# One list schedule for all five engines of a delta-rule attention with a routed MLP behind it, keys left unnormalised

## The chip, the cores and the metric

The kernel runs on one core of one Trainium2 chip. The metric is device time in microseconds (us) of one execution, lower is better. Inside the core five engines run side by side, each through its own list of instructions in order: PE (matrix multiplication), DVE (vector), ACT (scalar and activation), POOL and SP. SP does nothing here but issue DMA transfers; ACT and POOL issue some too. An instruction that waits for another engine holds up everything behind it in its own list.

## What is computed

The reference has two parts. The first is a linear attention with a delta rule, over 4 batches x 8 heads, 768 tokens and a head size of 48:

```
k_n = k / (norm(k) + 1e-6)
for t in range(S):
    y[t]  = q[t] @ state
    v_old = k_n[t] @ state
    state = state + beta[t] * outer(k_n[t], v[t] - v_old)
```

The second is a "mixture of depths" on the result x (each batch 768 rows of 384): a score per token, the 128 tokens with the highest score go through an MLP, and the gated result is added to them.

```
scores = x @ w_gate
top    = the 128 highest scores of the batch
ye     = relu(x[top] @ w1) @ w2            # 384 -> 1024 -> 384
out[top] = x[top] + sigmoid(scores[top])[:, None] * ye
```

## The kernel before

**The chunks.** The tokens are cut into chunks of 64. A *unit* is one chunk of two batches (16 heads); there are 24 units, 12 for batches 0 and 1 and 12 for batches 2 and 3. Within a chunk the delta rule is a triangular system, solved by an explicit inverse; from chunk to chunk it is a recurrence on the state.

**prep(i)**, per unit: ACT squares the keys (`ksq`, L195), DVE sums them (L197) and with ACT's square root makes 1/(norm + 1e-6) (`rn`, L199 to L202), POOL scales the keys (`kn`, L206), PE turns queries and keys (`p_t`, L214), ACT takes the turned blocks out of PSUM (`kq`, L216), PE makes the products k.k and k.q (`p_g`, L223). ACT takes the first out (`g`, L228), DVE takes the second out times a triangular mask (`pt`, L229), and SP shifts half of g to other partitions by DMA (L237).

**eliminate(e)**, for four units together (a *block*; six of them): DVE turns g (L245), scales it by beta (L247), POOL cuts it to a triangle (L249), and DVE inverts it in 30 steps of two dependent instructions (L256, L260), scales (L263) and turns the result into `tt` (L267) and back into g (L273). **join** puts the 32x32 inverses together to 64x64 ones (`p_z` L288, `p_j` L298, with copies by ACT, two units at a time).

**recur(i)**, per unit, in the order of the chunks: `r = v - k.state` (PE L326, DVE L329), `w = inverse.r` (PE L339, ACT `wbd` L344), the new state (PE L350, ACT `s` L356), the output `p_y` (PE L369, L376). For every second unit ACT takes the output out (`x`, L385), SP writes it, POOL multiplies it with w_gate (`xw`, L388) and ACT sums it to the score (L390).

**depths(g)**, for two batches: the scores are spread over all partitions (L404 to L423), DVE counts for every token how many are higher (L435, L440), and the tokens of rank below 128 are picked (L448 to L464), gathered, sent through the MLP (L483, L492; 256 tokens of the two batches side by side in L483) and added back by an indirect DMA (L496).

**Order.** The Python code advances four generators (rec, elim, prep, moe) in turn, with a fixed number of ticks per unit; the tile framework orders each engine's list and hands out the buffers of its pools. Ahead of everything ACT issues 96 small transfers of beta (L138). The last call, `depths(NG - 1)`, stands behind all units.

Of the kernel before, what the change touches and what calls it, by code (L numbers as in the profile page):

```python
# [8 lines left out]
FP32 = mybir.dt.float32  # L9
# [6 lines left out]
P = 128  # L16
C = 64
HC = 32


@with_exitstack
def kernel(
# [30 lines left out]

    nc = tc.nc
# [22 lines left out]
    loads = ctx.enter_context(tc.tile_pool(name="loads", bufs=3))  # L77
    small = ctx.enter_context(tc.tile_pool(name="small", bufs=3))
    work = ctx.enter_context(tc.tile_pool(name="work", bufs=2))
    keep = ctx.enter_context(tc.tile_pool(name="keep", bufs=8))  # L80
    moe = ctx.enter_context(tc.tile_pool(name="moe", bufs=2))
    psum = ctx.enter_context(tc.tile_pool(name="psum", bufs=1, space=PSUM))

    def ps_inv(name):
        return psum.tile([P, 512], FP32, name=name, tag="inv", bufs=3)

    units = [(g, c) for g in range(NG) for c in range(NCH)]
    n = len(units)
# [5 lines left out]
    raw = {}  # L94

    KB = 3
    qraw = [const.tile([P, HP, GB, DP], FP32, name=f"q_raw{m}") for m in range(KB)]
    NKN = 9
    kns = [const.tile([P, HP, GB, DP], FP32, name=f"kn{m}") for m in range(NKN)]

    def load(i, name):
        g, c = units[i]
        if name == "q":
            t = qraw[i % KB]
            dst = t.rearrange("p r b d -> p b r d")[:, :, :, :D]
# [35 lines left out]
    nbt = const.tile([P, NE, HC], FP32, name="nbt")  # L141
    nc.scalar.activation(nbt, bt, AF.Copy, scale=-1.0)

    ones = const.tile([P, P], FP32, name="ones")
    nc.vector.memset(ones, 1.0)
    mask_u = const.tile([P, C], FP32, name="mask_u")
    for par in range(2):
        hs = slice(par * C, (par + 1) * C)
        nc.gpsimd.affine_select(out=mask_u[hs], in_=ones[hs, :C], pattern=[[1, C]],
                                base=0, channel_multiplier=-1,  # L150
                                compare_op=ALU.is_gt, fill=0.0)
# [443 lines left out]
```

## Time and profile before

| what | value |
|---|---|
| median of three runs (lowest, highest) | 535.78 us (533.94, 540.02) |
| the profiled execution, its own time | 534.48 us |
| its span, first to last instruction | 532.8 us |
| mean granted TensorE clock | 0.784 of 2.4 GHz |
| busy share: PE, DVE, ACT, POOL | 61%, 50%, 31%, 16% |

The profiled execution lies 1.3 us under the median, and 1.7 us of its time lie outside the span. No engine is busy all the time, so the shares of the whole span say little; the stretches have to be read one by one. With the ends of the six L267 instructions as marks (137.8, 171.8, 231.2, 288.8, 359.8 and 422.1 us) the span falls into a start, five blocks and an end.

### The profile page before, as it was taken

To read this page: it belongs to the slowest core of one execution; us is meant where nothing else is said; L and a number is where in the kernel's file an instruction comes from. 1 tells how busy PE (TensorE), PEld (TensorE's weight loads), DVE (VectorE), ACT (ScalarE), POOL (GpSimd) and SP (SyncE) were. 2 spreads that over 40 slices of the span, in tenths; PEclk is the share of its full clock that TensorE was granted. 3 is DMA by queue.
4 is the path that set the end of the run, shared out by engine and by line. 5 is a ranking of instruction groups with operands and counts; after the bars stand their busy time and mean duration, and the time that the engine had idled before them with its cause. 6 is when DMAs were issued, how large, how long until landed. Compare 5 with 4: busy or idle time off the path is not lost.

```text
span 532.8 us, 13538 instructions
## 1 busy us (share of the span) xinstructions
PE 322.5 (61%) x5652; PEld 273.4 (51%) x5652; DVE 264.5 (50%) x722; ACT 166.8 (31%) x378; POOL 84.6 (16%) x126
## 2 busy tenths in 40 slices
PE   0000027650498898869882849489997578512594
PEld 0000015430487797758772648477786567411472
DVE  0000023689979257961978196981268800076100
ACT  0000045431335545533642425252434333300120
POOL 6000021201003212111212110220311101300002
PEclk9999999555569959965975576699969758856599
DMA  3462003333123433342333212211302300000002
GB/s 56 82 221 46 2 15 64 61 69 70 24 50 84 77 65 54 85 99 54 85 64 78 49 32 49 52 37 20 66 18 66 78 2 33 30 0 15 16 0 30
DMA packets 110957, 27.92 MB, mean 52 GB/s; under 512 B 105584, under 2 KB 110320, under 8 KB 110896
## 3 DMA queue, kind: packets, MB, share of 16 engines
q1 hardware_dynamic: 108912, 25.39, 23.0%
q0 software_dynamic: 832, 1.57, 1.7%
q8 instruction: 44, 0.72, 0.5%
q10 hardware_dynamic: 1152, 0.10, 0.1%
q14 instruction: 17, 0.14, 0.1%
HBM read 18.38 MB, written 5.51 MB: 45 GB/s over the span
## 4 chain that ended last, share of the span: by engine, by line
PE 39%; DVE 25%; issue 17%; ACT 7%; POOL 5%; DMA 4%; SPq 2%; POOLq 0%; DVEq 0%; ACTq 0%
DVE a_tmp L256 5%; PE p_y L376 5%; DVE a L260 5%; DVE junk_r L435 5%; PE p_m L483 4%; PE p_r L339 4%; PE p_j L298 4%; PE p_s L350 3%; PE p_m L492 3%; PE p_t L214 3%; PE p_z L288 3%; PE p_g L223 3%; PE p_y L369 2%; DMA k_raw<-in_k_dram 2%; PE p_m L416 2%
## 5 line engine op out<-in xcount | busy, mean ns | idle before, releaser
L256 DVE TENSOR_TENSOR a_tmp<-a 128x30 f32<-128x30 f32 (+9 forms) x180 | 67.3, 374 | 6.7 <-POOL a L249 2.8
L260 DVE TENSOR_TENSOR a<-a,a_tmp 128x30 f32<-128x30 f32 (+9 forms) x180 | 64.2, 357 | 4.4
L214 PE MATMUL p_t<-ident,kn 128*128 128x128 f32 x96 | 21.1, 353 | 74.1 <-POOL kn L206 69.1
L206 POOL TENSOR_TENSOR kn<-k_raw,rn 128x192 f32<-128x192 f32 x48 | 26.1, 565 | 209.2 <-PE p_s L350 76.7
L197 DVE TENSOR_REDUCE rn<-ksq 128x8 f32<-128x384 f32 x24 | 13.2, 549 | 85.7 <-ACT ksq L195 85.7
L214 PEld LDWEIGHTS p_t<-ident,kn 128*128 128x128 f32 x96 | 14.3, 179 | 79.4 <-POOL kn L206 70.7
L288 PE MATMUL p_z<-tt,g 32*32 32x32 f32 x768 | 22.3, 225 | 39.2 <-DVE tt L267 39.2
L229 DVE TENSOR_TENSOR pt<-p_g,mask_u 128x256 f32<-128x256 f32 x48 | 18.9, 417 | 54.4 <-PE p_y L376 36.5
L376 PE MATMUL p_y<-wbd,pt 128*64 128x96 f32 x384 | 44.4, 278 | 1.5 <-ACT wbd L344 1.5
L339 PE MATMUL p_r<-r,tt 64*64 64x48 f32 x704 | 33.0, 241 | 16.8 <-DVE r L329 14.4
L376 PEld LDWEIGHTS p_y<-wbd,pt 128*64 128x64 f32 x384 | 40.7, 162 | 3.0 <-ACT wbd L344 1.9
L223 PE MATMUL p_g<-kq 48*64 48x128 f32 x768 | 37.6, 327 | 7.1 <-ACT kq L216 7.1
L288 PEld LDWEIGHTS p_z<-tt,g 32*32 32x32 f32 x768 | 20.0, 139 | 40.6 <-issue 31.9
L339 PEld LDWEIGHTS p_r<-r,tt 64*64 64x64 f32 x704 | 29.0, 154 | 19.7 <-DVE r L329 16.3
L388 POOL TENSOR_TENSOR xw<-x,wg 128x384 f32<-128x384 f32 x24 | 25.0, 1042 | 88.6 <-ACT x L385 79.8
L344 ACT COPY wbd<-p_r 64x384 f32<-64x384 f32 x48 | 22.7, 473 | 50.0 <-PE p_r L339 37.4
L216 ACT COPY kq<-p_t 128x512 f32<-128x512 f32 x48 | 27.4, 586 | 32.4 <-PE p_t L214 30.1
L223 PEld LDWEIGHTS p_g<-kq 48*64 48x64 f32 x768 | 28.9, 163 | 12.8 <-ACT kq L216 10.6
L350 PE MATMUL p_s<-wbd,kn 128*48 128x96 f32 x352 | 24.9, 299 | 11.6 <-ACT wbd L344 11.6
L369 PE MATMUL p_y<-s,kq 48*64 48x48 f32 x704 | 31.8, 231 | 0.0
L329 DVE TENSOR_TENSOR r<-v_raw,p_r 128x384 f32<-128x384 f32 x22 | 12.1, 548 | 38.0 <-PE p_r L326 38.0
L298 PE MATMUL p_j<-g 32*32 32x32 f32 x768 | 25.2, 230 | 8.4 <-ACT g L292 8.3
(79 smaller groups left out, 536.7 us busy)
## 6 DMA issues: line engine op xcount, KB each, us to landing
k_raw<-in_k_dram SPq DMA_DIRECT2D x96, 48.0 KB
q_raw<-in_q_dram SPq DMA_DIRECT2D x96, 48.0 KB
v_raw<-in_v_dram SPq DMA_DIRECT2D x96, 48.0 KB
out_dram<-x SPq DMA_DIRECT2D x24, 192.0 KB
w_sb<-in_moe_w_dram SPq DMA_DIRECT2D x2, 1536.0 KB
bt<-in_beta_dram ACTq DMA_DIRECT2D x96, 1.0 KB
g<-g SPq DMA_DIRECT2D x48, 32.0 KB
tt<-tt SPq DMA_DIRECT2D x12, 128.0 KB
```

What stands on the lines that cost most here:

```text
L214: nc.tensor.transpose(ps[:, r * P:(r + 1) * P], x[:, r].rearrange("p b d -> p (b d)"), ident)
L216: nc.scalar.copy(kq[:, :, o], ps.rearrange("p (r t) -> p r t", t=P))
L223: nc.tensor.matmul(ps[bb][hs, r], lhsT=kq[ds, r, 0, hs], rhs=kq[ds, r, :, hs], start=True, stop=True)
L256: nc.vector.tensor_tensor(out=t, op=ALU.mult, in0=a[:, j + 1:, j:j + 1].to_broadcast([P, w, j]), in1=a[:, j:j + 1, :j].to_broadcast([P, w, ...
L260: nc.vector.tensor_tensor(out=a[:, j + 1:, :j], in0=a[:, j + 1:, :j], in1=t, op=ALU.add)
L288: nc.tensor.matmul(ps[lo[par], b], lhsT=gt[hi[par], n0 + b, :HC], rhs=tt[hi[par], n0 + b, HC:], start=True, stop=True)
L298: nc.tensor.matmul(ps[lo[par], b], lhsT=gt[lo[par], n0 + b, HC:], rhs=gt[lo[par], n0 + b, :HC], start=True, stop=True)
L339: nc.tensor.matmul(pw[hs, bb, r], lhsT=tt[hs, ch * GP + r * GB + bb], rhs=rhs[hs, bb, r], start=True, stop=True)
L350: nc.tensor.matmul(p_s[bb * DP:bb * DP + D, r], lhsT=kn[:, r, bb, :D], rhs=wb[:, bb, r].rearrange("p h d -> p (h d)"), start=(c == 0 and r ...
L369: nc.tensor.matmul(p_y[bb][rows, h * D:(h + 1) * D], lhsT=kq[ds, r, 1, par * C:(par + 1) * C], rhs=s_old[ds, r, par], start=(h == 0), stop ...
L376: nc.tensor.matmul(p_y[bb][rows, r * 2 * D:(r + 1) * 2 * D], lhsT=pt[:, r, bb], rhs=wb[:, bb, r].rearrange("p h d -> p (h d)"), start=(c = ...
L435: nc.vector.tensor_scalar(out=junk[:, :e - a], in0=rows[:, a:e], scalar1=mine, scalar2=None, op0=op, op1=ALU.add, accum_out=count[:, j, o: ...
```

## The change

The kernel is written anew round the same blocks of arithmetic.

**Order.** Every step is entered into a `Plan` with its engine, a duration written by hand (in us), the steps that it depends on, a priority (lower goes first) and the ring buffers that it takes and gives back. A list scheduler runs through the engines and yields one order, in which the instructions are then emitted, with the framework's own reordering off. Buffers are fixed rings; which slot a step gets is decided in the plan.

**Keys unnormalised.** No step scales the keys ahead. The turned block of k.k has the squared norms on its diagonal; `turn_in`, `root` and `scales` take them from there once per block. The factors go into the matrix before the elimination (`bh`), into a triangular table made by POOL (`mb`), and into the values (`vh`, a DVE instruction of 384 elements per unit). `ksq`, `rn` and `kn` are gone.

**Other moves.** The masked block p is copied out by ACT and masked in place by POOL, with two AFFINE_SELECT of 64 partitions x 512 elements per unit. join goes unit by unit. The score is one DVE instruction per output tile. `depths` goes batch by batch, its MLP 128 tokens wide, with the counting in two stages (tiles 0 to 3, then 4 and 5). Loads use two transfers instead of four. beta comes in 24 transfers, four of them (for the first block) from ACT behind three loads, the others from SP.

```diff
...
+    def add(self, eng, dur, emit, deps=(), prio=0.0, take=(), give=(), lat=0.15):
...
+    def pick(self, free, ops):
...
+        first = min(at for at, _ in cand)
+        urgent = [(at, op) for at, op in cand if op.prio < -500]
+        fits = [(at, op) for at, op in cand if at <= first + 1e-9 and
+                all(at + op.dur <= u + 0.2 or op.prio <= o.prio for u, o in urgent)]
+        return min(fits or urgent, key=lambda c: (c[1].prio, c[1].seq))
...
+            for name, key in op.take:
+                slots = self.rings[name]
+                k = min(range(len(slots)), key=lambda x: slots[x])
+                slots[k] = float("inf")
+                self.slot[key] = (name, k)
+            op.start, op.end = at, at + op.dur
+            free[op.eng] = op.end
...
+            for key in op.give:
+                self.refs[key] -= 1
+                last[key] = max(last.get(key, 0.0), op.end)
+                if self.refs[key] == 0:
+                    name, k = self.slot[key]
+                    self.rings[name][k] = last[key] + 0.15
...
+        return sorted(done, key=lambda o: (o.start, o.seq))
...
-                            nc.scalar.dma_start(
-                                out=bt[p0:p0 + GP, g * (NCH // BC) + e],
-                                in_=beta_src[par, half, g, e, c])
+    ring("k", 10, [GP, DP])
+    ring("q", 3, [GP, DP])
+    ring("v", 3, [GP, D])
+    ring("kq", 9, [GI, 2, P])
+    ring("p", 9, [GP, C])
+    ring("g", 2, [NB, C])
...
+    rings["inv"] = [psum.tile([P, 512], FP32, name=f"inv{m}") for m in range(3)]
+    plan.ring("inv", 3)
+    rings["y"] = [psum.tile([P, 2, 512], FP32, name="py")]
+    plan.ring("y", 1)
...
+    def load_beta(eng, e):
+        for par in range(2):
+            for half in range(2):
+                p0 = (par * 2 + half) * HC
+                eng.dma_start(out=bt[p0:p0 + HC, e],
+                              in_=beta_src[par, half, e // (NCH // BC), e % (NCH // BC)])
...
-        nc.scalar.activation(ksq, kr.rearrange("p b r d -> p (b r) d"), AF.Square)
-        rn = small.tile([P, GP], FP32, name="rn")
-        nc.vector.tensor_reduce(out=rn, in_=ksq, axis=AX.X, op=ALU.add)
-        nc.vector.tensor_scalar_max(rn, rn, 1e-30)
-        nc.scalar.activation(rn, rn, AF.Sqrt)
-        nc.vector.tensor_scalar_add(rn, rn, 1e-6)
-        nc.vector.reciprocal(rn, rn)
-        kn = kns[i % NKN]
-        for bb in range(GB):
-            nc.gpsimd.tensor_tensor(
-                out=kn[:, :, bb, :D], in0=kr[:, bb], op=ALU.mult,
-                in1=rn[:, bb * HP:(bb + 1) * HP, None].to_broadcast([P, HP, D]))
...
-            nc.vector.tensor_tensor(
-                out=pt[:, :, bb], in0=ps[bb][:, :, C:], op=ALU.mult,
-                in1=mask_u[:, None, :].to_broadcast([P, HP, C]))
+    def mask_p(i):
+        def emit():
+            t = got("p", i)
+            for par in range(2):
+                nc.gpsimd.affine_select(
+                    out=t[half[par]], in_=t[half[par]], pattern=[[0, GP], [1, C]], base=0,
+                    channel_multiplier=-1, compare_op=ALU.is_gt, fill=0.0)
...
+        parts = (("g", slice(0, 1), u), ("w", slice(1, 2), u + 31)) if first else \
+            (("g", slice(0, 2), u + 1),)
...
+        n["mp"] = pool(1.4, mask_p(i), [n["e", 1, 0], n["e", 1, 1]], u + 20)
+        n["sh"] = sp(1.3, shift(i), [n["e", 0, 0], n["e", 0, 1]], u, lat=2.5)
...
+        def scales():
+            nn, b = nrm[:, 1], bh[e % 2]
+            nc.vector.tensor_scalar(out=nn, in0=nrm[:, 0], scalar1=1e-6, scalar2=-1.0,
+                                    op0=ALU.add, op1=ALU.mult)
+            nc.vector.reciprocal(b, nn)
+            nc.vector.tensor_tensor(out=b, in0=b, in1=b, op=ALU.mult)
+            nc.vector.tensor_tensor(out=b, in0=b, in1=bt[:, e], op=ALU.mult)
+            nc.vector.transpose(out=nnT[e % 3], in_=nn)
...
+        def table():
+            nc.gpsimd.affine_select(
+                out=got("mb", e), in_=bh[e % 2][:, None, :].to_broadcast([P, HC, HC]),
+                pattern=[[1, HC], [-1, HC]], base=0, channel_multiplier=0,
+                compare_op=ALU.is_ge, fill=0.0)
...
+        def scale():
+            a = got("a", e)
+            nc.vector.tensor_tensor(out=a, in0=a, op=ALU.mult,
+                                    in1=bh[e % 2][:, :, None].to_broadcast([P, HC, HC]))
+            nc.vector.memset(a.rearrange("p i c -> p (i c)")[:, ::HC + 1], -1.0)
...
+        n["z"] = pe(0.95, z, [s["to"]], u, take=[key[0]])
+        n["ez"] = act(0.7, ez, [n["z"]], u, give=[key[0]])
+        n["j"] = pe(0.95, jj, [n["ez"], s["tb"]], u, take=[key[1]], give=[("g", e)])
+        n["ej"] = act(0.7, ej, [n["j"], s["mv"]], u, give=[key[1]])
...
+        def vh():
+            t = got("v", i)
+            nc.vector.tensor_tensor(
+                out=t, in0=t, op=ALU.mult,
+                in1=nnT[e % 3][:, ch * GP:(ch + 1) * GP, None].to_broadcast([P, GP, D]))
...
+        n["lv"] = sp(1.3, load(i, "v"), prio=10 * i - 25, take=[("v", i)], lat=2.2)
+        r["vh"] = dve(0.57, vh, [n["lv"], N["e", e]["sc"]], u - 8)
+        x = r["vh"]
+        if c > 0:
+            r["r"] = pe(0.75, mm_r, [o["es"], o["w1"]], u)
+            r["sub"] = x = dve(0.57, sub, [r["r"], r["vh"]], u, give=[("v", i)])
+        r["w"] = pe(0.95, mm_w, [x, n["ej"], s_mv(e), o.get("w1")], u,
+                    give=[("tt", e)] + ([("v", i)] if c == 0 else []))
...
+        for par in range(2):
+            r[f"w{par}"] = act(0.42, out_w(par),
+                               [r["w"], prev2.get("p"), prev2.get("s")], u)
+        if c < NCH - 1:
+            r["s"] = pe(0.75, mm_s, [r["w0"], r["w1"], o.get("es"), prev2.get("es")], u)
+            r["es"] = act(0.48, out_s, [r["s"], o.get("q1"), o.get("r")], u)
+        yt = dict(take=[yk]) if c % 2 == 0 else {}
...
+            yt = {}
+        last = r["p"] = pe(0.7, mm_p, [r["w0"], r["w1"], n["mp"], r.get("q1")],
+                           10 * i + 6, give=[("kq", i), ("p", i)], **yt)
...
+                N["score", b, j] = dve(0.65, score(bb), [xo, N["wg"]], 10 * i + 12,
+                                       give=[("x", i, bb)])
...
+        for j0, j1 in stages:
...
+            dg = pool(0.3 + 0.13 * w, diag(j0, j1), sc, u, take=[("sel", b, j0)] + [("rep", b)] * (j0 == 0))
...
+            for j in range(j1):
+                a = 0 if j >= j0 else j0
+                n = j1 - a
+                last = j0 > 0 and j == j1 - 1
+                counts.append(dve(0.3 * (3 if a <= j else 1) + 0.13 * n, ranks(j, a, j1),
+                                  [er, eo] + counts[-1:], u + 1,
+                                  give=[("rep", b)] if last else []))
...
+        ch = dve(1.2, choose, [counts[-1], N.get("chosen")], u, take=[("sel", b, "s")])
...
+    for i in range(NU):
+        prep(i)
+    for e in range(NE):
+        eliminate(e)
+    for i in range(NU):
+        recur(i)
+    for b in range(B):
+        depths(b, 10 * NCH * (b // GB + 1) + 5 + 40 * (b % GB), 15)
+    with tc.manual_schedule(engines=None):
+        constants()
+        plan.emit()
```

Where the table of steps puts the instructions shows best at three places.

ACT's list from its start, up to the first copies, before (`ksq`, `rn`: squared keys and norms; `bt`: beta; `kq`: turned keys and queries):

```order
L138 DMA bt<-in_beta_dram 8x1x32 x96
L195 ACT_TABLE_LOAD
L195 ACTIVATE ksq<-k_raw 128x384
L142 ACTIVATE nbt<-bt 128x192
L216 COPY kq<-p_t 128x4x128
L195 ACTIVATE ksq<-k_raw 128x384
```

and now:

```order
L324 DMA k_62<-in_k_dram 64x8x48 x2
L324 DMA k_64<-in_k_dram 64x8x48 x2
L324 DMA q_72<-in_q_dram 64x8x48 x2
L251 DMA bt<-in_beta_dram 32x1x32 x4
L339 ACT_TABLE_LOAD
L339 COPY kq_77<-inv_112 128x4x128
L339 COPY kq_78<-inv_113 128x4x128
```

The 96 transfers of beta are gone from here; ten transfers stand ahead of the first copy, and nothing for norms stands between the copies.

POOL's list from the first preps on, before (`kn`: scaled keys; `a`: the matrix of the elimination):

```order
L206 TENSOR_TENSOR kn_83<-k_raw,rn 128x4x48 x2
L206 TENSOR_TENSOR kn_84<-k_raw,rn 128x4x48 x2
L249 AFFINE_SELECT a<-a 128x1024
L251 MEMSET a 128x32
L206 TENSOR_TENSOR kn_85<-k_raw,rn 128x4x48 x2
```

and now (`p`: the block of k.q that is masked, `mb`: the table for a block's elimination):

```order
L369 AFFINE_SELECT p_87<-p_87 64x512 x2
L369 AFFINE_SELECT p_88<-p_88 64x512 x2
L441 AFFINE_SELECT mb_99<-bh_134 128x1024
L369 AFFINE_SELECT p_89<-p_89 64x512 x2
L369 AFFINE_SELECT p_90<-p_90 64x512 x2
```

The scaling of the keys has gone, and the masking of p, from DVE, has come; the table is one instruction of 128x1024 per block, as L249 was.

PE's list behind the first block's elimination, before (`p_z`, `p_j`: join; `p_r` from v or r: w; `p_s`: state; `p_y`: output; `p_t`, `p_g`: prep of a later unit):

```order
L288 MATMUL p_z<-tt_231,g 32x32 x32
L298 MATMUL p_j<-g 32x32
L288 MATMUL p_z<-tt_231,g 32x32 x9
L298 MATMUL p_j<-g 32x32 x31
L288 MATMUL p_z<-tt_231,g 32x32 x23
L339 MATMUL p_r<-v_raw,tt_231 64x48
L298 MATMUL p_j<-g 32x32 x32
L214 MATMUL p_t<-ident,q_raw_78 128x128 x4
L339 MATMUL p_r<-v_raw,tt_231 64x48 x15
L214 MATMUL p_t<-ident,kn_87 128x128 x4
L350 MATMUL p_s<-wbd_227,kn_79 48x96 x8
L376 MATMUL p_y<-wbd_227,pt 64x96 x8
```

and now (`prec`: r and w, `psta`: state, `py`: output; the `inv` banks hold join and prep):

```order
L514 MATMUL inv_112<-tt_100,g_95 32x32 x16
L514 MATMUL inv_113<-tt_100,g_95 32x32 x16
L514 MATMUL inv_114<-tt_100,g_95 32x32 x16
L525 MATMUL inv_112<-g_95 32x32 x16
L525 MATMUL inv_113<-g_95 32x32 x16
L525 MATMUL inv_114<-g_95 32x32 x16
L574 MATMUL prec<-v_74,tt_100 64x48 x16
L514 MATMUL inv_112<-tt_100,g_95 32x32 x16
L588 MATMUL psta<-wbd_139,k_61 48x96 x8
L525 MATMUL inv_113<-g_95 32x32 x16
L562 MATMUL prec<-s_141,kq_78 64x48 x16
L611 MATMUL py<-wbd_139,p_86 64x96 x8
```

The first w stands behind three units' worth of p_z and p_j pieces of 16, and no prep stands between the first units; preps of later units follow behind.

## Rows read from the trace of the kernel before

**Rows 1.** Busy time by stage; columns in the first line.

```profile
core 0: us, PE busy (x) PEld busy (x) DVE busy (x) ACT busy (x) POOL busy (x), PEclk, DMA share, GB/s
0.00:69.30 69.30, 1.09 (x4) 0.72 (x4) 0.63 (x4) 0.00 (x0) 8.68 (x30) 1.00 0.31 78
69.30:137.80 68.50, 28.82 (x316) 21.05 (x316) 45.66 (x128) 24.66 (x58) 12.00 (x22) 0.68 0.31 55
137.80:422.10 284.30, 227.78 (x4522) 198.43 (x4522) 192.27 (x508) 119.43 (x270) 51.81 (x64) 0.78 0.30 59
422.10:458.00 35.90, 28.29 (x685) 26.58 (x686) 3.62 (x4) 11.93 (x26) 2.00 (x2) 0.71 0.08 21
458.00:532.80 74.80, 36.50 (x128) 26.64 (x126) 22.31 (x80) 10.78 (x25) 10.11 (x8) 0.72 0.08 16
```

**Rows 2.** Waits: who for whom, us in total, times, longest.

```profile
ACT L195 <- DMA bt<-in_beta_dram: 69.3, 1, 69.3
```

**Rows 3.** Timeline of the start: start us, us, engine line op, count.

```profile
0.80 11.55 ACTq L138 DMA_DIRECT2D bt<-in_beta_dram  x16
...
69.33 1.28 ACT L195 ACT_TABLE_LOAD   x1 [69.33 <-DMA bt<-in_beta_dram]
...
95.47 1.30 SPq L237 DMA_DIRECT2D g<-g  x2
...
99.04 1.93 DVE L245 STREAM_TRANSPOSE a<-g 128x1024 f32<-128x1024 f32 x1
```

**Rows 4.** Groups of instructions: count | busy us, mean ns | idle before.

```profile
L256 DVE TENSOR_TENSOR a_tmp<-a 128x30 f32<-128x30 f32 (+9 forms) x180 | 67.3, 374 | 6.7 <-POOL a L249 2.8
L260 DVE TENSOR_TENSOR a<-a,a_tmp 128x30 f32<-128x30 f32 (+9 forms) x180 | 64.2, 357 | 4.4
...
L435 DVE TENSOR_SCALAR_CACHE_REDUCE junk_r<-rep,own 128x128 bf16<-128x128 f32 (+5 forms) x44 | 28.4, 646 | 2.1 <-ACT rep L423 1.3
L216 ACT COPY kq<-p_t 128x512 f32<-128x512 f32 x48 | 27.4, 586 | 32.4 <-PE p_t L214 30.1 <-PE p_y L369 2.0
...
L229 DVE TENSOR_TENSOR pt<-p_g,mask_u 128x256 f32<-128x256 f32 x48 | 18.9, 417 | 54.4 <-PE p_y L376 36.5 <-ACT g L228 17.8
L228 ACT COPY g<-p_g 128x256 f32<-128x256 f32 x48 | 15.6, 372 | 20.0 <-PE p_g L223 19.5
...
L197 DVE TENSOR_REDUCE rn<-ksq 128x8 f32<-128x384 f32 x24 | 13.2, 549 | 85.7 <-ACT ksq L195 85.7
...
L440 DVE SCALAR_TENSOR_TENSOR junk_r<-rep,own,tri 128x128 bf16<-128x128 f32 x24 | 9.5, 398 | 0.5
```

**Rows 5.** Timeline of DVE and POOL round POOL's L249, second block.

```profile
131.19 0.27 DVE L256 TENSOR_TENSOR a_tmp<-a 128x108 f32<-128x108 f32 x1
131.35 1.27 POOL L249 TENSOR_SCALAR_AFFINE_SELECT a<-a 128x1024 f32<-128x1024 f32 x1 [9.44 <-DVE a L247]
131.49 1.23 DVE L260 TENSOR_TENSOR a<-a,a_tmp 128x108 f32<-128x108 f32 x1
```

**Rows 6.** Timeline of PE, one unit at the full clock.

```profile
158.88 1.13 PE L339 MATMUL p_r<-r,tt 64*64 64x48 f32 x32 [0.18 <-DVE r L329]
...
161.97 1.48 PE L376 MATMUL p_y<-wbd,pt 128*64 128x96 f32 x16
...
164.87 0.66 PE L214 MATMUL p_t<-ident,q_raw 128*128 128x128 f32 x4
```

**Rows 7.** Timeline of PE in the end stretch.

```profile
422.15 1.92 PE L288 MATMUL p_z<-tt,g 32*32 32x32 f32 x64 [5.06 <-DVE tt L267]
...
433.21 1.94 PE L339 MATMUL p_r<-r,tt 64*64 64x48 f32 x30 [1.26 <-ACT tt L302]
...
466.10 1.01 DVE L435 TENSOR_SCALAR_CACHE_REDUCE junk_r<-rep,own 128x768 bf16<-128x768 f32 x1 [0.44 <-ACT rep L423]
...
502.80 12.89 PE L483 MATMUL p_m<-xeT,w_sb 128*128 128x256 f32 x48 [0.57 <-ACT xeT L474]
...
515.53 10.48 PE L492 MATMUL p_m<-w_sb,hT 128*128 128x384 f32 x32
```

More of the change, by code (lines that the diff above doesn't have):

```diff
@@ L87, with sbuf, ring @@
-    units = [(g, c) for g in range(NG) for c in range(NCH)]
-    n = len(units)
+    psum = ctx.enter_context(tc.tile_pool(name="psum", bufs=1, space=PSUM))
+    def sbuf(name, shape, dt=FP32):
+        return const.tile([P] + shape, dt, name=name)
+    plan = Plan()
+    rings = {}
+    def ring(name, count, shape, dt=FP32):
+        rings[name] = [sbuf(f"{name}{m}", shape, dt) for m in range(count)]
+        plan.ring(name, count)
+    ring("k", 10, [GP, DP])
+    ring("q", 3, [GP, DP])
+    ring("v", 3, [GP, D])
@@ new lines, with got, maker, add @@
+    plan.ring("y", 1)
+    prec = psum.tile([P, 2, 512], FP32, name="prec")
+    psta = psum.tile([P, GI, 2 * D], FP32, name="psta")
+    def got(*key):
+        name, m = plan.live[key]
+        return rings[name][m]
+    def maker(eng):
+        def add(dur, emit, deps=(), prio=0.0, take=(), give=(), lat=0.15):
+            return plan.add(eng, dur, emit, deps, prio,
+                            [(t[0] if isinstance(t, tuple) else t, t) for t in take],
+                            give, lat)
+        return add
@@ new lines @@
+    pe, act, dve, pool, sp = [maker(e) for e in ("PE", "ACT", "DVE", "POOL", "SP")]
+    bt = sbuf("bt", [NE, HC])
+    beta_src = beta.rearrange("(g bb) (r par) (e c half t) -> par half g e c (bb r) t",
+                              bb=GB, par=2, half=2, t=HC, c=BC)
+    def load_beta(eng, e):
[4 more added lines that the diff above has]
+                              in_=beta_src[par, half, e // (NCH // BC), e % (NCH // BC)])
@@ new lines, in load_w @@
+    def load_w(what, t):
+        if what == 0:
+            nc.sync.dma_start(out=wg, in_=bass.AP(
+                tensor=moe_w_gate.tensor, offset=moe_w_gate.offset,
+                ap=[[0, P]] + [list(x) for x in moe_w_gate.ap]))
+        elif what == 1:
+            nc.sync.dma_start(out=w1_sb[:, t], in_=moe_w1[t * P:(t + 1) * P])
+        else:
+            nc.sync.dma_start(out=w2_sb[:, t:t + 2], in_=moe_w2[t * P:(t + 2) * P]
+                              .rearrange("(t p) f -> p t f", p=P))
@@ L141 @@
[L141 to L151, printed above, removed]
@@ new lines, with turn, emit, out @@
+    N = {}
+    def turn(i, o, nm):
+        def emit():
+            x, ps = got(nm, i), got("inv", i, nm)
+            for r in range(GI):
+                nc.tensor.transpose(ps[:, r * P:(r + 1) * P],
+                                    x[:, 2 * r:2 * r + 2].rearrange("p b d -> p (b d)"),
+                                    ident)
+        def out():
+            nc.scalar.copy(got("kq", i)[:, :, o],
+                           got("inv", i, nm).rearrange("p (r t) -> p r t", t=P))
+        return emit, out
@@ L498, in depths @@
                 out_offset=bass.IndirectOffsetOnAxis(ap=idx[b][:, 0:1], axis=0),
-                in_=oe, in_offset=None, compute_op=ALU.add)
-            yield
-    running = {}
-    def advance(key, times=1):
-        for _ in range(times):
-            gen = running.get(key)
-            if gen is not None and next(gen, running) is running:
-                del running[key]
-    def finish(key):
-        while key in running:
-            advance(key)
-    loaded = {0: {"k", "q"}, 1: {"k", "q"}}
```

889 lines of the change are left out of this document (504 added, 385 removed).

## The prediction

> **What bounds the kernel now.** I read the busy table by stage first, then the waits, then the timeline of each stage's start. The table [rows 1] shows three different kernels. For 69.3 us nothing but POOL's clearing and four matmuls happens: 13% of the span. The waits name one releaser for all of it, the beta transfers that stand ahead of ACT's first instruction [rows 2]; the timeline has ACT issuing 16 of the 96 in 11.55 us, 0.72 each, and 96 x 0.72 is 69 [rows 3]. From there to 137.8 DVE and PE take turns on the first preps and the first elimination. In the five blocks from 137.8 to 422.1 PE is busy 80% and DVE 68% of 284.3 us, at a mean granted clock of 0.78 [rows 1]: neither is full, each waits for the other. From 422.1 on DVE has no elimination left, and the last four units, the ranking of two batches and their MLP follow each other for 110.7 us. So 248 of 533 us lie ahead of and behind the blocks, where single chains decide, and 284 in the blocks, where the order does.
>
> **The start.** The change takes 92 of 96 transfers off ACT and the norms out of the first preps. ACT now issues ten transfers: 0.8 + 10 x 0.72 = 8.0 us. The table load of 1.28 follows [rows 3], then four copies of 0.59 and eight of 0.37 [rows 4], 5.3 us, with two hand-overs to PE between (2 us, my estimate): 16.6. On SP a load of two transfers stands ahead of the last shift of two, 0.65 each [rows 3]: 19.2; a shift that left at 96.77 was there for the turn-in at 99.04, so 2.3 us on: the first turn-in comes at about **22 us** instead of 99.04. Ends: 18, with no hand-over seen and the load off the way, and 37.7, if the path from ACT's release to the turn-in stays the 29.7 us of before. I take 22, since the loop over ACT, DVE and POOL for the norms, which fills most of the 29.7, has no instruction left.
>
> The first elimination took 38.7 us of before, from 99.04 to 137.8. Between its steps stood DVE's share of four preps, one L197 of 0.55 and two L229 of 0.42 each [rows 4], 5.6 together, now gone. In come three vh, passes over 384 elements like L197's; I take 0.45 a piece, since independent instructions overlap by some 0.1. With 0.5 for the norm steps: **35 us**, without the lock of the next part.
>
> **The lock of POOL.** The trace shows what a POOL AFFINE_SELECT does to the elimination [rows 5]: DVE's step of 108 elements, 0.27 in the row ahead, takes 1.23 while POOL's 1.27 us instruction runs; 0.96 is lost. Before, there were six such, put mostly into DVE's own wait. Now POOL runs 48 of half the columns, two per unit, nearly all while DVE eliminates, and six tables of 128x1024. By proportion a mask takes 0.64 and, with the same 0.31 hidden, costs 0.33: 48 x 0.33 + 6 x 0.96 = 22 us on DVE. The scaling of keys and scores on POOL, which met the same steps before and is in the means of L256 and L260, goes; that is the credit, which no row prices. I take a net of 12, 2 per elimination; the ends are 0 (the credit cancels all) and 54 x 1.27 = 69 (each blocks for the whole of the only length shown).
>
> The Trainium skill, page "SBUF — State Buffer", section "SBUF: two separate sides", says that the port pair shared by DVE and GpSimd is an exclusive lock, so that an instruction of two SBUF inputs on DVE stands still for the whole of a GpSimd instruction that reads SBUF. The row agrees but for 0.31 us; by the rule taken whole the sum would carry 48 x 0.64 + 6 x 1.27 = 38 for 22. That is a rival below.
>
> **The five blocks.** DVE per block: 35 less the three vh (1.4), plus the turn back into g, which like the turn-in is 1.93 [rows 3], plus four vh and four subtractions at 0.45, plus the lock's 2: 41 us, 205 for five. On top come 16 of the 24 scores, which POOL and ACT did before, 16 x 0.55 = 9, and the ranking of two batches: the counts were 28.4 + 9.5 over four batches [rows 4], 9.5 each, and the two stages add four instructions per batch of at most 0.65, so 12; twice, with the selection, 25. DVE's floor is 239. PE has to fit under it. One unit at the full clock: from w to the first transposes of the next stands 6.0 us [rows 6], with 1.3 for transposes and 1.0 for its join (half of the 64 that took 1.92 at the low level [rows 7], twice, at the full clock) 8.3: 33 per block, 42 at the 0.78 of before. That is level with DVE's 41 to 48, so some waiting stays, above all since the plan writes mm_p at 0.7 where the trace has 1.48 [rows 6] and knows nothing of the lock: whoever is late holds its list. I take 2 us per block: **249** for 284.3 of before. ACT loses squares, roots and accumulations and gains the copies of p, 48 x 0.37 = 18 [rows 4]; at 119 busy of 284 us it covers that. SP issues half as many loads and 20 transfers of beta, 13 us at 0.65 spread over 250. Neither adds to the sum.
>
> **The end.** From 110.7: the first w came 11.1 us after the last inverse [rows 7], by halves of the block; unit by unit I expect 5 (-6). The way from the last output at 458.0 to the first count at 466.10 [rows 1, 7] had POOL, ACT and POOL again in it; now one score on DVE and a spread already prepared, 3 (-5). The MLP of the second batch now falls among the last four units: half of 12.89 plus half of 10.48 [rows 7], 11.6, of which 8 lie on PE's path (+8). Of the last two batches only one MLP stands behind the last count (-11.7), but PE finishes the other before it takes up the last selection, 8 after the counts are done (+8). More counts and less waiting for the second spread about cancel (+1). That gives **105**.
>
> **Sum.** 22 + 35 + 249 + 105 = 411, and the 1.7 us outside the span make 412.7. The profiled run was 1.3 under the median, too little to move it: **413 us**, 23% under 535.8.
>
> **The rivals.** *The order written out from wrong durations.* Lists in a fixed order wait in turn, and a block costs what it did, 284.3 / 5 = 56.9: 22 + 35 + 284 + 105 + 1.7 = 448. For it: PE's need of 42 is at DVE's, and mm_p is off by half. Against: PE was 80% busy in blocks of 57, and DVE loses no work to preps it must wait for. Chance 0.2.
>
> *The lock at full length.* The masks stop DVE for their whole time and no credit comes back: by the proportion of the row 48 x 0.64 + 6 x 1.27 = 38 for my net of 12, 439. Chance 0.12. The rule of the skill named above asks for it; the only row that shows the form has 0.31 less.
>
> *No waiting.* PE stays at 2.4 GHz because its gaps are filled, DVE never waits, the credit cancels the lock (239 - 10), the end loses 7: 22 + 35 + 229 + 98 + 1.7 = 386. In the trace the clock fell whenever PE idled before a join, and each block still begins with one. Chance 0.1.
>
> *The start stays.* If not the number of beta transfers but their landing or the keys' held the start, some 60 us come back: 475. The waits name the transfers, and their issue alone fills the time. Chance 0.02.
>
> *PE at the low level throughout, slower than before.* At 1.2 GHz a unit is 16.6, a block 66, and copies of w and state that PE now waits for, with no prep between the units, some 9 more: 75. 22 + 35 + 375 + 125 + 1.7 = 559. It decides once the mean of the blocks' granted clock falls under some 0.55; the trace has 0.78 there with more gaps than the new order leaves. Chance 0.03.
>
> **How the numbers follow.** My forecast has 0.53, and its own range is 395 to 432, from the start's ends and the lock's. To leave out no more than 2 in 10 the range takes in the lock, the fixed order and no waiting, with 1% at either end: **382 to 452**. A measurement of this kernel tells 1% from no change. Faster by over 1%: all but the last rival, 0.96; slower 0.03; within 1% 0.01.
>
> **What would show it.** In the profile after, the first L423 (turn-in) near 22, the ends of L471 (the inverses) near 57, 99, 143, 187, 243 and 306; ACT's first copy near 9 to 10; steps L458 and L462 with means above 0.374 and 0.357 and single ones over 0.6 beside L369; DVE busy over 85% in the blocks; 105 from the last L471 to the end. Wrong would be: a turn-in behind 30, blocks of 55 with DVE waiting for L562 or L574, steps no slower beside L369, or an end stretch over 115.

## The result, and the profile after

The changed kernel took **440.89 us** (median of 4 runs, 440.69 to 445.83) against 536.52 (533.94 to 540.02) for the kernel before: a ratio of 0.824, 95% interval 0.816 to 0.831. The profiled run took 440.75, span 439.0. The forecast was 413, the range 382 to 452. The first table shows the stages, cut at the first turn-in (L423) and at the end of each inverse (L471); it answers to [rows 1].

```profile
core 0: us, PE busy (x) PEld busy (x) DVE busy (x) ACT busy (x) POOL busy (x), PEclk, DMA share, GB/s
0.00:29.55 29.55, 15.37 (x256) 12.47 (x256) 3.84 (x20) 10.25 (x21) 5.97 (x18) 0.92 0.67 104
29.55:66.64 37.09, 16.39 (x200) 13.02 (x200) 34.42 (x75) 12.24 (x32) 10.38 (x13) 0.59 0.64 146
66.64:110.09 43.45, 38.35 (x896) 34.39 (x896) 35.88 (x82) 21.48 (x55) 8.97 (x9) 0.77 0.45 89
110.09:160.64 50.55, 42.78 (x960) 38.62 (x960) 39.23 (x94) 22.96 (x59) 7.90 (x9) 0.77 0.42 87
160.64:205.11 44.47, 39.82 (x856) 34.42 (x856) 36.66 (x87) 22.52 (x57) 9.77 (x11) 0.84 0.39 77
205.11:264.48 59.37, 43.07 (x896) 37.96 (x896) 44.33 (x118) 21.58 (x56) 7.84 (x11) 0.71 0.22 44
264.48:326.15 61.67, 47.73 (x847) 41.95 (x847) 47.73 (x136) 18.54 (x42) 4.22 (x3) 0.72 0.17 38
326.15:439.00 112.85, 82.10 (x973) 69.41 (x973) 37.49 (x137) 24.96 (x59) 9.91 (x10) 0.76 0.11 25
```

Against the sum of the prediction the start is 7.5 longer (29.6 for 22), the first elimination 2.1 (37.1 for 35), the five blocks 10.5 (259.5 for 249) and the end 7.9 (112.9 for 105): 28 in all, spread over every term. In the blocks DVE is busy 203.8 of 259.5 us (the sum of five rows), so 55.7 are idle, and PE 211.8: shares of 79% (I expected over 85%) and 82%. Who waits for whom, in us, times and the longest, answers to [rows 2]:

```profile
DVE r L566 <- PE prec L562: 41.5, 21, 6.6
DVE a L423 <- DMA g<-g: 24.5, 1, 24.5
DVE junk L632 <- ACT x L618: 21.6, 4, 16.1
DVE idx L754 <- PE inv L749: 11.6, 2, 9.6
...
PE inv L514 <- DVE tt L471: 52.2, 6, 13.7
```

The beta transfers are gone from the list. What is left is a ping-pong: PE stands before each join until the inverse is there, up to 13.7 at a time, and DVE, its list written out, stands at 21 of the 22 subtractions of the recurrence (L566) until PE has its operand. The start, in the timeline that answers to [rows 3]:

```profile
4.29 5.35 SPq L324 DMA_DIRECT2D q<-in_q_dram  x4
...
6.58 3.65 ACTq L251 DMA_DIRECT2D bt<-in_beta_dram  x4
...
10.26 1.28 ACT L339 ACT_TABLE_LOAD   x1 [10.26 <-DMA q<-in_q_dram]
...
17.02 8.11 SPq L380 DMA_DIRECT2D g<-g  x6
...
21.14 1.34 ACTq L324 DMA_DIRECT2D q<-in_q_dram  x2
...
26.65 1.49 SPq L380 DMA_DIRECT2D g<-g  x2
...
29.55 1.90 DVE L423 STREAM_TRANSPOSE a<-g 128x1024 f32<-128x1024 f32 x1 [24.47 <-DMA g<-g]
```

ACT issues until 10.2, 2.2 behind my sum, copies from 11.55 on, and ends its last copy for the shifts at 19.9, 3.3 behind the sum. SP issues the last shift from 26.65 to 28.14, and that end lies 8.9 behind my 19.2; the turn-in begins 1.4 later. Of SP's own waits up to there, the longest for a transfer is this one, ahead of the third unit's shift:

```profile
SPq L380 <- DMA q<-in_q_dram: 3.3, 1, 3.3
```

ACT's copies for that shift were done at 18.3. The records of the trace show the transfers of SP and ACT sharing eight completion semaphores in turn, and each transfer waiting until the one before it on the same semaphore has landed. The third shift follows the load of q that ACT issues at 21.14, and that load lands at 23.8. The elimination's steps and the masks answer to [rows 4, 5]:

```profile
L458 DVE TENSOR_TENSOR tmp<-a 128x30 f32<-128x30 f32 (+9 forms) x180 | 67.6, 376 | 5.6
L462 DVE TENSOR_TENSOR a<-a,tmp 128x30 f32<-128x30 f32 (+9 forms) x180 | 66.1, 367 | 6.2
...
L369 POOL TENSOR_SCALAR_AFFINE_SELECT p<-p 64x512 f32<-64x512 f32 x48 | 36.0, 751 | 144.0 <-ACT p L361 142.7
```

133.7 us for the steps, where before had 131.5: the masks' lock (DVE and POOL holding each other up) and the credit for the POOL work that went nearly cancel. Last the end, by the timeline, with what answers to [rows 7]:

```profile
363.14 5.43 PE L794 MATMUL inv<-w_sb,hT 128*128 128x384 f32 x16
...
373.16 0.56 DVE L632 SCALAR_TENSOR_TENSOR junk<-x,wg 128x384 bf16<-128x384 f32 x1 [16.05 <-ACT x L618]
...
399.33 0.96 DVE L742 TENSOR_TENSOR sel<-iota_r,rank 128x768 f32<-128x768 f32 x1
...
408.34 1.40 PE L749 MATMUL inv<-tok,sel 128*128 128x2 f32 x12
...
414.55 1.00 POOL L764 DMA_INDIRECT xe<-out_dram,idx  x1 [3.51 <-DMA out_dram<-oe,idx]
...
419.21 7.93 PE L780 MATMUL inv<-xeT,w_sb 128*128 128x128 f32 x48 [0.62 <-ACT xeT L774]
```

PE takes the MLP of batch 1 (to 368.6) ahead of the last units' outputs, and DVE stands 16 us for the last scores. The selection of batch 3 is ready at 400.3, but PE first ends batch 2's MLP: 8.0 lost, as forecast. Then the gather of batch 3 waits for batch 2's scatter, which I had not seen: the indices are there at 410.0, it leaves at 414.55.

### The profile page after: what moved, and what is told of

Same layout as the page of the kernel before. It is cut to its first block, busy times and chain, and to the rows that moved or that the text cites. A ratio compares the mean times of both kernels' runs of the same rounds, so it can differ in the third digit from the quotient of the medians.

```text
span 439.0 us, 13687 instructions
## 1 busy us (share of the span) xinstructions
PE 325.6 (74%) x5884; PEld 282.2 (64%) x5884; DVE 279.6 (64%) x741; ACT 154.5 (35%) x381; POOL 65.0 (15%) x84
## 5 line engine op out<-in xcount | busy, mean ns | idle before, releaser
L458 DVE TENSOR_TENSOR tmp<-a 128x30 f32<-128x30 f32 (+9 forms) x180 | 67.6, 376 | 5.6
L462 DVE TENSOR_TENSOR a<-a,tmp 128x30 f32<-128x30 f32 (+9 forms) x180 | 66.1, 367 | 6.2
L514 PE MATMUL inv<-tt,g 32*32 32x32 f32 x768 | 22.8, 235 | 52.2 <-DVE tt L471 52.2
L369 POOL TENSOR_SCALAR_AFFINE_SELECT p<-p 64x512 f32<-64x512 f32 x48 | 36.0, 751 | 144.0 <-ACT p L361 142.7
L611 PE MATMUL py<-wbd,p 128*64 128x96 f32 x384 | 44.6, 280 | 0.0
L352 PE MATMUL inv<-kq 48*64 48x128 f32 (+1 forms) x896 | 36.5, 293 | 7.8 <-ACT p L361 4.6
L580 ACT COPY wbd<-prec 64x384 f32<-64x384 f32 x48 | 22.7, 473 | 55.7 <-PE prec L574 50.4
L611 PEld LDWEIGHTS py<-wbd,p 128*64 128x64 f32 x384 | 40.2, 161 | 2.5 <-issue 1.4
L566 DVE TENSOR_TENSOR r<-v,prec 128x384 f32<-128x384 f32 x22 | 12.2, 554 | 41.6 <-PE prec L562 41.5
L729 DVE TENSOR_SCALAR_CACHE_REDUCE junk<-rep,own 128x256 bf16<-128x256 f32 (+4 forms) x60 | 31.8, 530 | 2.0
L574 PE MATMUL prec<-r,tt 64*64 64x48 f32 x704 | 32.7, 253 | 0.0
L574 PEld LDWEIGHTS prec<-r,tt 64*64 64x64 f32 x704 | 29.6, 168 | 1.5 <-issue 0.6
L601 PE MATMUL py<-s,kq 48*64 48x48 f32 x704 | 30.1, 235 | 0.0
L335 PE MATMUL inv<-ident,k 128*128 128x128 f32 x96 | 18.3, 324 | 14.0 <-DMA k<-in_k_dram 6.6
```

The source lines that it names most:

```text
L352: nc.tensor.matmul(bank(i, w, rt)[half[par], r, o], lhsT=kq[ds[rt], r, 0, half[par]], rhs=kq[ds[rt], r, o, half[par]], start=True, stop=True)
L369: nc.gpsimd.affine_select(out=t[half[par]], in_=t[half[par]], pattern=[[0, GP], [1, C]], base=0, channel_multiplier=-1, compare_op=ALU.is_ ...
L458: nc.vector.tensor_tensor(out=t, op=ALU.mult, in0=a[:, j + 1:, j:j + 1].to_broadcast([P, w, j]), in1=a[:, j:j + 1, :j].to_broadcast([P, w, ...
L462: nc.vector.tensor_tensor(out=a[:, j + 1:, :j], in0=a[:, j + 1:, :j], in1=t, op=ALU.subtract)
L514: nc.tensor.matmul(ps[lo[par], b], lhsT=g[hi[par], n0 + b, :HC], rhs=tt[hi[par], n0 + b, HC:], start=True, stop=True)
L574: nc.tensor.matmul(pw[half[par], a % 2, a // 2], lhsT=tt[half[par], ch * GP + a], rhs=x[half[par], a], start=True, stop=True)
```

## The experiments

Every ratio is to the kernel before, run on the same chip. In x2 and x8 to x12 the lines from L423 on stand 7 further down (L566 is L573).

**x1: beta alone, in the kernel before.**

```diff
...
-    nbt = const.tile([P, NE, HC], FP32, name="nbt")
-    nc.scalar.activation(nbt, bt, AF.Copy, scale=-1.0)
...
+    load_beta(nc.scalar, 0)
...
     def eliminate(e):
+        nc.scalar.activation(nbt[e], bt[e], AF.Copy, scale=-1.0)
+        if e + 1 < NE:
+            load_beta(nc.sync, e + 1)
```

> The kernel before, with one part of the change: only block 0's 16 of the 96 beta transfers stay on ACT ahead of its work, the other 80 go to SP, 16 at the start of each elimination. If the issue of the transfers is what held the start, 80 x 0.72 = 58 us go: 479 us against 536.5, so the start alone is 58 of the 96 us gained, and the rest of the change has some 38. If the keys' landing or the norms held it, the time stays over 520. If SP's 80 issues (52 us in all) hold up the loads and shifts of the blocks, part of the 58 comes back there: 485 to 500.

507.1 us (505.2 to 508.5), ratio 0.945 (0.940 to 0.950): 31 of the 96, not 58. Its stages, to the turn-in, the first inverse and the second, and PE's longest wait (L213 is L214 before):

```profile
0.00:50.40 50.40, 21.50 (x205) 15.77 (x205) 10.43 (x39) 15.48 (x35) 14.43 (x42) 1.00 0.51 119
50.40:84.52 34.12, 11.06 (x117) 8.46 (x116) 29.38 (x77) 6.57 (x16) 3.58 (x6) 1.00 0.28 47
84.52:131.84 47.32, 38.58 (x812) 33.94 (x809) 36.28 (x91) 19.89 (x47) 7.03 (x10) 0.98 0.33 60
```

```profile
PE p_t L213 <- DMA q_raw<-in_q_dram: 37.8, 5, 12.4
```

The turn-in comes at 50.4 for 99.04, 48.6 sooner, and the first elimination takes 4.6 less. The blocks take 25 of that back, 13.3 in the first alone (47.3; before, 34.0 between the same two inverses), where the preps of the next block used to be ahead. PE waits 37.8 us for loads of q, 9.7 before. So the time lies outside all three of my cases, 7 above the third, which is nearest in kind: the wait for beta had been covering loads and preps, and the loads are late next. That SP's 80 more issues do it, and not the missing lead, was not separated.

**x2: the start's transfers in another order.** The preps of the first block are split in two, and everything that isn't needed for its turn-in waits for its last shift. The loads of q and beta go to SP, so six of ACT's ten transfers go too.

```diff
-        n["lq"] = kq_on[0](1.3, load(i, "q", kq_on[1]), prio=u - 20, take=[("q", i)], lat=2.2)
+        late = [N[BC - 1]["sh"]] if part == 1 or not first else []
...
+            n["lq"] = sp(1.3, load(i, "q"), late, prio=u - 20, take=[("q", i)], lat=2.2)
...
+    N["beta", 0] = sp(2.6, lambda: load_beta(nc.sync, 0), prio=-63, lat=2.5)
```

> The changed kernel with the start's transfers in another order: k of the first block, beta, the four shifts, and only then q, v, the weights and the loads of later blocks; all else the same. If it was SP's queue of loads ahead of the shifts that put the first turn-in at 29.6 where I had 22, it now comes at 18 to 20 and the time falls by 8 to 11, to 430 to 433. If the chain of copies and products on ACT and PE holds it, the turn-in stays at 26 or later and the time at 438 to 441. If the blocks wait for what now loads later, the turn-in comes early but the time stays.

438.4 us (434.3 to 439.9), ratio 0.817 (0.813 to 0.822). The turn-in does come at 20.1, 9.4 sooner. ACT's last copy for the shifts ends 2.7 sooner, at 17.2, and the last shift leaves SP right behind it; the other 6.7 are what the order of the transfers on SP had held. The time hardly follows. The timeline shows a part of what gives it back:

```profile
20.14 1.90 DVE L430 STREAM_TRANSPOSE a<-g 128x1024 f32<-128x1024 f32 x1 [15.06 <-DMA g<-g]
...
23.53 0.59 ACT L339 COPY kq<-inv 128x512 f32<-128x512 f32 x1 [6.37 <-PE inv L335]
...
25.69 0.18 DVE L440 TENSOR_SCALAR nrm<-nrm 128x32 f32<-128x32 f32 x1 [3.43 <-ACT nrm L436]
```

ACT's list has a copy of q ahead of the square root of the norms, q lands late, and DVE stands 3.4 us at the head of its critical chain. The first elimination takes 41.3 for 37.1, so the 9.4 are 5.2 by its end. By its signs this is the third of my cases, the turn-in early and the time nearly the same, but it is the first elimination and not the blocks that gives back most. The profiled run ended 6.8 sooner (span 432.2), the median is 2.5 lower, which is less than these runs tell apart.

**x3: two priorities in the end.**

```diff
-        mi = pe(1.4, mm_idx, [ch], u, take=[("inv", b, "idx")], give=[("sel", b, "s")])
+        mi = pe(1.4, mm_idx, [ch], u - 30, take=[("inv", b, "idx")], give=[("sel", b, "s")])
...
-        u += du
+        u += du + 40 * (b == 1)
```

> The changed kernel with two priorities changed: the MLP of batch 1 goes behind the last units' outputs on PE, and the selection product of batch 3 ahead of batch 2's MLP. If PE's list holds the end, the last scores come some 10 us sooner (the wait of 16.1 at L632 goes to about 6) and the gather of batch 3 leaves 8 to 12 us sooner, ahead of the scatter of batch 2: 441 - 18 = 423, the end stretch 95. If DVE's counts are what the end hangs on and the MLP of batch 1 merely moves into their cover, only one of the two pays: 430 to 433. If neither: 439 to 441.

430.6 us (427.6 to 433.9), ratio 0.804 (0.799 to 0.809). The end stretch is 101.1 for 112.9. Both moves worked: the last score starts at 362.4, not 373.8, and the last gather at 397.1, not 414.6, ahead of the scatter. Yet the time is that of my second case, in which only one of them pays, because a third thing took part of it back:

```profile
DVE own L717 <- PE inv L711: 12.9, 4, 6.2
```

2.9 before: the small products that fetch the own scores of batches 2 and 3 now stand behind the MLP of batch 1 on PE, and the counts behind them.

**x4: no masks.**

```diff
-        n["mp"] = pool(1.4, mask_p(i), [n["e", 1, 0], n["e", 1, 1]], u + 20)
+        n["mp"] = pool(1.4, lambda: None, [n["e", 1, 0], n["e", 1, 1]], u + 20)
```

> The changed kernel in the very same order without the 48 POOL masks (L369), so the values of p that lie on the wrong side of the diagonal are left in. It prices the lock. In the trace DVE's steps lose 12.5 us beside L369. If DVE's loss is on the path, 441 - 12 = 429; if DVE's waits for PE take it up, as its 56 idle us in the blocks suggest, 437 to 441; if a mask stopped DVE for its whole 0.75 on the path, 441 - 36 = 405.

429.7 us (428.1 to 435.4), ratio 0.798 (0.793 to 0.803): 11.2 less by the medians, 10.4 by the profiled runs, as in my first case. The steps' groups:

```profile
L458 DVE TENSOR_TENSOR tmp<-a 128x30 f32<-128x30 f32 (+9 forms) x180 | 61.5, 342 | 5.6
L462 DVE TENSOR_TENSOR a<-a,tmp 128x30 f32<-128x30 f32 (+9 forms) x180 | 59.8, 332 | 6.2
```

121.3 for 133.7: 12.4 us of DVE's work was standing still beside masks, 0.26 for each of the 48, and nearly all of it showed in the time, though DVE was idle for 56 us in the blocks. The 0.26 is a mean: by the trace of the changed kernel 13 of the 48 ran beside no step at all (four were done before the elimination began), so it is 0.35 for each of the other 35. One pair of masks and the steps beside it, and two such steps in x4:

```profile
44.08 1.51 POOL L369 TENSOR_SCALAR_AFFINE_SELECT p<-p 64x512 f32<-64x512 f32 x2 [3.65 <-ACT p L361]
44.38 0.69 DVE L458 TENSOR_TENSOR tmp<-a 128x198 f32<-128x198 f32 x1
45.10 0.70 DVE L462 TENSOR_TENSOR a<-a,tmp 128x198 f32<-128x198 f32 x1
```

```profile
43.13 0.37 DVE L458 TENSOR_TENSOR tmp<-a 128x198 f32<-128x198 f32 x1
43.53 0.37 DVE L462 TENSOR_TENSOR a<-a,tmp 128x198 f32<-128x198 f32 x1
```

The first elimination falls from 37.1 to 33.5, the blocks from 259.5 to 251.7. The Trainium skill, page "SBUF — State Buffer", section "SBUF: two separate sides", lets such a DVE instruction stand for the whole of POOL's, which would be up to the masks' 36.0; a third of that was measured. The trace agrees in kind: the step at 44.38 begins with 0.48 of the first mask left (it ends at 44.86) and loses 0.32, and the pair costs the two steps 0.65 of its 1.51. Idle time is no cushion when it lies behind a wait: PE's wait for the inverses falls from 52.2 to 44.2 without the masks, and the blocks shrink by as much.

**x5 and x6: the plan's PE durations.** x5 has three of them at the full clock, x6 all at the trace's means.

```diff
...
-        last = r["p"] = pe(0.7, mm_p, [r["w0"], r["w1"], n["mp"], r.get("q1")],
+        last = r["p"] = pe(1.53, mm_p, [r["w0"], r["w1"], n["mp"], r.get("q1")],
```

> The changed kernel with three of the plan's PE durations set to what the traces show at the full clock: w 1.14 (0.95), s 0.86 (0.75), p 1.53 (0.7). Nothing else is touched, the plan orders anew. If the lists wait because the plan took PE's work for shorter than it is, DVE's waits for L562 (41.5 in all, 33.7 of them in the blocks) fall by a third or more and the time with them: 426 to 431. If the waits belong to the recurrence itself, whatever the lists, the time stays within 1%: 437 to 445.

444.3 us (442.9 to 445.1), ratio 0.829 (0.824 to 0.833), within the second case.

> The changed kernel with all of the plan's PE durations set to the means of its own trace, that is at the granted clock of 0.75 (p 1.86, w 1.52, s 1.19 and so on). If exact durations make a good order, the waits for L562 fall below 20 and the time to 415 to 425. The rival: with PE that slow the plan itself puts the third elimination 41 us later (its own end is then 440 where it was 362), DVE idles meanwhile, and the time is 445 to 465.

472.4 us (470.6 to 475.8), ratio 0.881 (0.875 to 0.887), above both cases. My explanation for the waits found no support. In x5 those at L566 do shrink by a fifth:

```profile
DVE r L566 <- PE prec L562: 32.2, 14, 7.1
```

but the blocks still take 258.7 and the end 115: PE's wait for the inverse grew to 57.3. In x6 the plan puts the third and fifth eliminations far back, and blocks of 80 and 38 alternate. Truer durations of PE did not make a better list; those of DVE and ACT, and the lock, were left as they were.

**x7: no precedence for the recurrence.**

```diff
-        u = -1000 + 10 * i
+        u = 10 * i
```

> The changed kernel without the recurrence's precedence in the plan (priority 10 i, where it has 10 i - 1000); the same instructions in another order. The plan's own forecast is 28 us more. If the order is what the blocks hang on, the chip shows that too: 465 to 475. If it is the work that was taken out (norms, scalings, square roots) and any order that keeps the engines fed does, the time stays within 2%: 433 to 450.

459.4 us (456.9 to 465.7), ratio 0.854 (0.848 to 0.860), 18.5 more with the same instructions. The blocks take 36 more (295.7), the end 16 less, since less is left for it.

```profile
PE inv L514 <- DVE tt L471: 102.9, 6, 25.1
```

PE's wait for the inverses doubles from 52.2. The new order also lets DVE stand 40.1 us at L554 for loads of v, where the changed kernel has 1.5, so the 18.5 are the price of this order as a whole. Between my two cases, nearer to the order than to none.

**x8: x2 and x3 together.**

> The start's order of x2 and the end's priorities of x3 together. If they are independent, 441 - 3 - 10 = 428; the turn-in 9 us sooner should show in full where the blocks don't give it back: then 421 to 424.

425.3 us (422.3 to 426.9), ratio 0.791 (0.786 to 0.796): nearly additive, between my two figures, and a base for what follows.

**x9 to x11: where the rankings stand.**

```diff
-        depths(b, 10 * NCH * (b // GB + 1) + 5 + 40 * (b % GB), 15)
+        depths(b, {0: 125, 1: 200, 2: 245, 3: 285}[b], 15)
```

x10 has 170 and 205 for the first two, x11 the products of L718 at u - 60.

> The kernel of x8 with the ranking of batch 1 moved: its priority puts it behind the last elimination, among the last four units, where DVE was idle for 33 of 47 us. In the changed kernel the last elimination began 26 us after the one before, with the ranking in between. If DVE's list sets the last block, its 61 us fall to some 50 and the ranking costs nothing in the end: 425 - 11 = 414. If PE, busy 48 of those 61, sets it, the block falls by 4 at most and the end grows by as much: 423 to 427.

402.6 us (401.4 to 403.6), ratio 0.748 (0.744 to 0.753): more than either case. The last block and the end, of x8 and then of x9:

```profile
260.91:322.03 61.12, 47.21 (x847) 41.52 (x847) 47.66 (x136) 18.57 (x42) 4.15 (x3) 0.75 0.18 38
322.03:424.90 102.87, 81.71 (x973) 69.53 (x973) 37.46 (x137) 24.80 (x59) 9.96 (x10) 0.75 0.12 27
```

```profile
256.75:312.00 55.25, 48.31 (x847) 42.41 (x847) 42.11 (x113) 18.64 (x42) 4.19 (x3) 0.75 0.19 42
312.00:399.60 87.60, 76.52 (x973) 64.39 (x973) 41.91 (x162) 24.79 (x59) 10.59 (x10) 0.81 0.15 32
```

The block gives 5.9, half of what DVE's list promised: PE, busy 48 of 55, is the next candidate. The end gives 15.3 although DVE has more to do there: the new list has the own products and spreads ahead of the MLPs, so the 12.6 us at L724 in x8 are gone (under 1 is left), and the last count ends 19.8 after the last score begins, not 29.4. PE's granted clock there is 0.81 for 0.75, and its 973 matmuls are busy 5.2 less; how much of the 15.3 that is was not separated.

> As x9, with the ranking of batch 0 behind the last elimination too, so that the MLPs of both batches lie in the end. By DVE's list blocks 4 and 5 fall to some 48 each and the end keeps its 101: 400 to 405. By PE, which gets another MLP of 13 us into an end where it is busy 82 of 113, the end grows by 10 and 412 to 418 come out.

402.8 us (401.0 to 413.6), ratio 0.747 (0.741 to 0.753), the same. The last two blocks fall to 49.7 and 47.7, the end grows to 102.4 with PE busy 91.4: so the time, the blocks and the end are those of the first case. Against x9, though, the end is 14.8 longer and PE busy 14.9 more in it: with the MLPs of batches 0 and 1 both there, PE's work counts, as in the second.

> As x9, with the four products that fetch a batch's own scores (L718) also 60 earlier in priority, since DVE waited 12.6 for them in x8, 6.2 at a time behind the MLP of batch 1. If that wait lies on the end's path, 6 to 10 less than x9; if the counts after it only start sooner to wait for the same spread copies, the same as x9 within 1%.

401.6 us (400.5 to 404.5), ratio 0.748 (0.742 to 0.753): no difference, as x9 had already lost that wait.

**x12: the square root ahead of the copies of q.**

```diff
-            n["lq"] = sp(1.3, load(i, "q"), late, prio=u - 20, take=[("q", i)], lat=2.2)
+            n["lq"] = sp(1.3, load(i, "q"), late, prio=u - 20, take=[("q", i)], lat=6 if first else 2.2)
```

> The kernel of x11 with one number changed: the plan takes the landing of the first block's q for 6 us instead of 2.2, so that ACT's square root of the first norms stands ahead of the copies of q. In x2 the first elimination took 41.3 where the changed kernel had 37.1, with DVE waiting 3.4 for that root while ACT waited for a copy of q. If that is what the start gave back, the wait goes, the first elimination takes 38 and the time falls by 3, to 398 or 399. If the plan's other shifts outweigh it, 400 to 405.

**398.06 us** (394.7 to 401.4, 6 runs), ratio 0.741 (0.736 to 0.745): the best, 10% under the changed kernel. The root comes at once:

```profile
21.98 0.23 ACT L436 ACTIVATE nrm<-nrm 128x32 f32<-128x32 f32 x1 [3.82 <-DVE nrm L432]
22.24 0.18 DVE L440 TENSOR_SCALAR nrm<-nrm 128x32 f32<-128x32 f32 x1 [0.29 <-ACT nrm L436]
```

The first elimination takes 38.8, turn-in at 19.8; so the ordered copy was most of what the first elimination of x2 had lost, 2.5 of the 4.2 over the changed kernel. The 3.5 against x11 is as expected, though at 1% it is what a measurement can just tell.

## Why the prediction was right, and where it was off

Side and range were right because the parts it rested on held: the start's wait was ACT's queue, the first elimination and the end stay near what they were, the blocks shrink by a tenth. The value missed by 28 us in four terms.

**The start (22, measured 29.6).** The step that failed is "On SP a load of two transfers stands ahead of the last shift". Before that shift SP issues 16 transfers of k, q and v from 4.29 on besides six of the shifts, and stands between them until earlier loads have landed, 3.3 us of it ahead of the third unit's shift. ACT's chain is a smaller miss, 3.3 late at its last copy, 2.2 of that in its issue. x2 moves the loads behind the shifts and shortens ACT's list, and the turn-in comes at 20.1. x1 shows a second flaw: I put all of the start's gain down to the transfers. In the old structure that part alone is worth 31, since loads and preps had been done under cover of the wait. The other 65 come with the rest of the change; taking the recurrence's precedence out of the plan costs 18.5 (x7). The remaining 46 or so have no run of their own: how much the unnormalised keys bring was not tried.

**The first elimination (35, measured 37.1).** The masks account for it: 33.5 without them. That my 35 lies so near is partly luck, as the next part shows.

**The blocks (249, measured 259.5).** Two steps failed against each other. DVE's floor was 239 and is 204 busy. The 41 per block rest on the 38.7 from 99.04 to 137.8, which I took for DVE's work. That stretch holds more than I took out of it:

```profile
128.05 1.91 DVE L245 STREAM_TRANSPOSE a<-g 128x1024 f32<-128x1024 f32 x1
130.05 1.22 DVE L247 TENSOR_TENSOR a<-a,nbt 128x1024 f32<-128x1024 f32 x1
```

These two belong to the next block; the small instructions of the norms (L199 to L202) are 3.3, and 2.3 are idle. That is 8.7 a block, 44 in five, and the net of 10 for the lock in the blocks was 8 too high as well. Against them, a vh took 0.61 and a subtraction 0.55 where I had 0.45; the smaller terms were not followed up. And the 2 us of waiting per block are 11, 55.7 in five. PE's term held: 42 per block in the sum, 42.4 busy. "Level with DVE's [...], so some waiting stays" was too small a price: here two engines at 80% that hand to each other in a fixed order wait by turns, and what x4 takes out of one such wait comes out of the time. So a floor 35 too high and waits 46 too short left a miss of 10.5. My first rival named such waits but gave wrong durations as their cause; x5 and x6 do not bear that out, and x7 and x9 show that what stands where counts. The waits at L566 stayed between 32 and 42 in every version of the changed kernel but x6 and x7, so what would remove them is open.

**The lock (net 12, measured 2).** The masks cost 12.4 on DVE and 11.2 of time (x4), where I had 48 x 0.33 = 16; the other 6 of my 22 were for the tables, which x4 leaves in. Without the masks the steps are 10.2 under the 131.5 of before [rows 4], which is the size of the credit that I put at 10. That the old POOL work is what those steps carried fits, but no run took it out of the kernel before.

**The end (105, measured 112.9).** The 8 us for the last selection were exact. The MLP of batch 1, which I priced at 8 on PE's path, stood ahead of the last outputs and cost DVE a wait of 16.1 for the last scores, and the gather behind a scatter was not in the sum. x3 gained 10 by these two; in x9 the end is 15 shorter than in x8, by what stood behind them.

The other rivals: the lock at full length gave nearly the measured time, 439, by a mechanism that x4 rules out, so that nearness is chance; PE's granted clock was 0.71 to 0.84 in the blocks, so neither the case without waiting nor that at 1.2 GHz came.

## What to carry to other kernels

When a long wait goes, ask what else ran under its cover before counting all of it as gain: 49 us at the start were worth 31 in the end. With orders written out ahead, the largest gain (22.8 of 42.8 us here) came from moving a whole side task to where its engine is idle, and with it what stood ahead of the last counts, not from truer durations. A stretch's length is not an engine's work: before it is reused as a cost, its idle time and what it holds of other steps have to come out. Idle time on an engine is no cushion for a slowdown if the idle time is a wait that the slowdown feeds.

## What the runs showed of the hardware

A POOL AFFINE_SELECT of 64x512, 0.67 us at the median, cost DVE's two-input steps 0.26 each on average over 48 (x4), 0.35 over the 35 that ran beside a step. It works both ways: one of POOL's took 1.68, begun beside DVE's L468 of 1.23. In this program a transfer of SP or ACT did not leave before the one ahead of it on its completion semaphore had landed, whichever engine had issued that one: a shift on SP stood 3.3 us for a load that ACT had issued.
